# Widening six of 36 weight pieces in the last layer's first block instead of during the experts, and leaving out four unused products of the attention

## The chip, the cores and the metric

One core of a Trainium2 chip. The metric is the device time of one launch in microseconds (us), lower is better. The five engines are named as the profile names them: PE (TensorE, with PEld for its weight loads), DVE (VectorE), ACT (ScalarE), POOL (GpSimd) and SP (SyncE, which here only issues transfers). Each runs its own queue of instructions in order.

## What is computed

Three layers follow one another: a recurrence over 768 positions for 4 sequences and 8 heads of 48 (called the attention), a mixture of 8 experts that takes the best expert of each token, and a gated layer of width 1536.

```python
for t in range(S):                                    # attention
    y[:, :, t] = einsum(r_t, state + u * k_t v_t)
    state = w * state + k_t v_t
for e in range(8):                                    # experts, 384 -> 1024 -> 384
    h = maximum(x[mask] @ w1[e], 0)
    out[mask] = gate_w * eom * (h @ w2[e])
g = x @ w_gate                                        # last layer, 384 -> 1536 -> 384
out = (g * sigmoid(g) * (x @ w_val)) @ w_out
```

The three weight matrices of the last layer arrive as float64. They are 36 pieces of 128 x 384 (12 slices of the width, three matrices each).

## The kernel before

**Attention.** 24 tiles of 128 tokens (6 per sequence), software pipelined, in an order written by hand. For tile `i`, `scaled_k` puts four products in POOL's queue, in this order: two that make `ck` (L455, L456), `kdT` (L458) and `kdc` (L459). `ck` is summed by DVE (`cb`, L478), from `cb` ACT builds the diagonals `dsb` (L482), and PE uses them. `kdc` is read only by `state(i)`, which returns at once for the last tile of a sequence. Loads run three tiles ahead and wait until the tile's buffer has been read.

**Experts.** After the attention a scheduler orders the instructions of each engine by its own estimate of times and by their priority in the program. A step `(e, f)` is 9 products `ph` (x by w1) and, two steps later (`LAG`), 9 products `py` (h by w2). ACT makes the high half of `h` (L1207) and DVE the low half (L1208). Two banks hold `ph`, so the `ph` of step f+2 waits for DVE's `h` of step f. Each step also splits half a group of the raw weights in high and low (ACT L1060, DVE L1063). Expert 0's first 256 tokens are done ahead of the loop (`head`), so that its 8 steps in the loop have only 160 tokens, and a shorter DVE sum `hs` (L1205). From step 10 on, every other step takes a stage of `sorted_positions` (sort tables; DVE L729 to L753, POOL L744 and L749).

**Widening.** `MoE.widen` is a generator. For one piece it loads the two 32-bit halves of each float64 (`cva`, 384 KB), makes a float32 with two ACT operations (L1020, L1021), five of DVE (L1025, L1027, L1030, L1033, L1034) and one of POOL (L1031), and stores it to the DRAM tensor `m32` (L1024, L1040). Three `next` make a piece. `filler(FILLN)` draws two per expert step from step `FILL0` on, and `filler(1000)` draws what is left in step (7, 0).

**Last layer.** `FFN.prepare` is called in step (7, 0). It loads pieces from `m32` (`rw`, L1291) and splits them (L966, L967); `FFN.run` works on blocks of 512 tokens and 12 slices `f`. In the first block slice f+3's pieces are split at slice f. A slice is 18 products `pg` and `pv` (L1356), a sigmoid on ACT (L1360), two DVE products (L1361, L1362), the split of the result in `hh` and `hl` (L966, L967) and 12 products `po` (L1323), which stand on PE behind the `pg` and `pv` of a later slice. The inputs of block 1 go to the pool `xq2`, which is empty during block 0.

Of the kernel before, what the change touches and what calls it, by code (L numbers as in the profile page):

```python
# [9 lines left out]
F32 = mybir.dt.float32  # L10
# [28 lines left out]
def moe_kernel(ctx, tc, cst, small, tok, tr, u, w1, w2, m_gate, m_val, m_out, out):  # L39
# [68 lines left out]
    moe = MoE(tc, outer, env)  # L108
# [197 lines left out]
    with ExitStack() as actx:  # L306
# [132 lines left out]
        def scaled_k(i):  # L439
# [19 lines left out]
            nc.gpsimd.tensor_tensor(out=kdc[:, :, 0:D], in0=k_t, in1=wk_tok, op=ALU.mult)  # L459
# [511 lines left out]
class MoE:  # L971
    def __init__(self, tc, c, env):
# [6 lines left out]
        self.stages = self.widen()  # L979
# [12 lines left out]
    def widen(self):  # L992

        nc, env, cv = self.nc, self.env, self.cv
        DM, KD = env["DM"], env["KD"]
        def load(i):
            a = cv.tile([P, 2 * DM], I32, name="cva", bufs=3)
            f, kind = divmod(i, 3)
            if kind < 2:
                src = (env["m_gate"], env["m_val"])[kind].bitcast(I32).rearrange("(k p) f -> p k f", p=P)  # L1000
                nc.sync.dma_start(
                    out=a.rearrange("p (k f) -> p k f", k=KD), in_=src[:, :, 2 * f * P : 2 * (f + 1) * P]
                )
            else:
                nc.sync.dma_start(out=a, in_=env["m_out"].bitcast(I32)[f * P : (f + 1) * P, :])
            return a

        n = self.F32CH
        loaded = [load(0), load(1)]
        yield  # L1010
        store = None
        for i in range(n):
            if i + 2 < n:
                loaded.append(load(i + 2))
            pair = loaded.pop(0).rearrange("p (n t) -> p n t", t=2)
            ab = cv.tile([P, DM], F32, name="ab", bufs=3)
            bits = ab.bitcast(I32)
            low = cv.tile([P, DM], F32, name="low")
# [7 lines left out]
            ex = cv.tile([P, DM], I32, name="exw")  # L1026
# [11 lines left out]
            if i + 1 < n:  # L1038
                yield
        nc.sync.dma_start(out=env["m32"][n - 1], in_=store)  # L1040
# [196 lines left out]
class FFN:  # L1237
# [25 lines left out]

    def scales(self, ns):
# [6 lines left out]
    def x_tiles(self, n):  # L1271
        start, size = self.blocks[n]
        xh, xl = (self.xq[n % 2].tile([P, self.env["KD"], size], F32R, name=name) for name in ("xh2", "xl2"))
        self.xs[n] = xh, xl, self.scales(slice(start, start + size))
# [28 lines left out]
    def run(self):  # L1303
# [4 lines left out]
        self.xq.append(c.enter_context(tc.tile_pool(name="xq2", bufs=1, reuse_waits="tile")))  # L1308
        self.wts = c.enter_context(tc.tile_pool(name="wts", bufs=1, reuse_waits="tile"))
# [32 lines left out]
        for n, (_, size) in enumerate(blocks):  # L1342
            xh, xl, _ = self.xs.pop(n)
            po = [p_o.tile([P, DM], F32, name=f"po{t}") for t in (range(2, 4) if n == len(blocks) - 1 else range(size // P))]
            for f in range(KF2):
# [20 lines left out]
                if n == 0 and f + self.AHEAD < KF2:  # L1366
                    with tc.issue_after(a), tc.issue_after(b):
                        self.weights(f + self.AHEAD)
                    if f + self.AHEAD + 1 < KF2:
# [26 lines left out]

LAG = 2
# [4 lines left out]
FILL0, FILLN = 2, 2  # L1402
# [98 lines left out]
```

## Time and profile before

| | |
|---|---|
| median of 3 runs | 820.76 us (820.52 to 821.94) |
| the profiled execution, its own time | 828.89 us |
| span in the trace of that execution | 827.1 us |
| PE busy | 790.2 us, 96% |
| DVE busy | 515.1 us, 62% |
| ACT busy | 347.6 us, 42% |
| POOL busy | 210.6 us, 25% |

The profiled execution has its own time, 8.1 us above the median of the runs, and its span covers all but 1.8 us of that. In the trace the attention goes to about 130 us, the head of expert 0 to 150, the loop over the experts from 156 to 370, and the last layer from 370 to 823. An engine's share over the whole span mixes these stages, so the stages are read one by one. PE's busy time is modelled for overlapping products: a busy PE is not PE at its peak.

### The profile page before, as it was taken

The numbers are of one execution on the slowest core, as the hardware profiler recorded it, in microseconds if no ns is written. First come the engines' busy times: TensorE is split into PE (matmuls) and PEld (weight loads), VectorE is DVE, ScalarE is ACT, GpSimd is POOL, SyncE is SP. The second block draws the span as 40 slices with busy tenths as digits, with TensorE's granted clock in tenths as the row PEclk, the third lists the DMA queues.
The fourth block names the chain that finished last, engine by engine and source line by source line (L and its number), as shares of the span: only waits on it lengthen the run. The fifth ranks groups of instructions, "written<-read, shape, count | busy, mean of one in ns | idle before, by whom it ended". The sixth has DMA issues, their size and how long they took to land.

```text
span 827.1 us, 15617 instructions
## 1 busy us (share of the span) xinstructions
PE 790.2 (96%) x5982; PEld 718.5 (87%) x5983; DVE 515.1 (62%) x1091; ACT 347.6 (42%) x791; POOL 210.6 (25%) x207
## 2 busy tenths in 40 slices
PE   7989779699999999999999999999999999999997
PEld 4877678688999999998888888888888888889997
DVE  7789997399999999955554335333533443344443
ACT  5878663364575576554432222212222222122322
POOL 6999951354524422200001000200020020001000
PEclk9999999899999999999999999999999999999999
DMA  8899933686777877342210000000000010001000
GB/s 322 297 361 334 332 128 108 215 268 194 253 222 260 252 245 253 89 139 86 86 59 32 19 1 13 39 0 1 14 39 1 0 45 1 1 7 40 1 20 24
DMA packets 61860, 99.28 MB, mean 120 GB/s; under 512 B 5461, under 2 KB 48105, under 8 KB 61776
## 3 DMA queue, kind: packets, MB, share of 16 engines
q1 hardware_dynamic: 58320, 88.34, 32.3%
q0 software_dynamic: 3456, 9.85, 3.5%
q8 instruction: 49, 0.80, 0.4%
q14 instruction: 35, 0.29, 0.1%
HBM read 81.64 MB, written 16.53 MB: 119 GB/s over the span
## 4 chain that ended last, share of the span: by engine, by line
issue 58%; PE 16%; DVE 4%; POOL 3%; DMA 1%; ACT 1%; POOLq 0%; SPq 0%; ACTq 0%; DVEq 0%
PE ph L1188 7%; PE py L1188 6%; POOL out_dram L1332 2%; PE pya L1188 1%; DMA m<-ab 1%; PE pha L1188 1%; DVE w2l L1063 1%; PE pt L1154 1%; DVE ab L1034 1%; DMA cva<-in_w_gate_dram 0%; DVE exw L1027 0%; PE ph L1184 0%; DVE ab L1030 0%; DVE h L1208 0%; DVE low L1033 0%
## 5 line engine op out<-in xcount | busy, mean ns | idle before, releaser
L1361 DVE TENSOR_TENSOR hv<-pg,hv 128x512 f32<-128x512 f32 (+1 forms) x84 | 51.6, 615 | 153.8 <-ACT hv L1360 153.7
L1332 POOL DMA_INDIRECT out_dram<-ot,tokd x24 | 24.8, 1035 | 448.3 <-DVE ot L1331 443.6
L1360 ACT ACTIVATE hv<-pg 128x512 f32<-128x512 f32 (+1 forms) x84 | 45.1, 537 | 167.4 <-PE pg L1356 167.2
L966 ACT CAST hh<-hv 128x512 fp32r<-128x512 f32 (+1 forms) x84 | 47.0, 560 | 142.1 <-DVE hv L1362 142.1
L1323 PE MATMUL po<-wh,hl 128*128 128x384 f32 x288 | 96.8, 337 | 0.0
L1323 PE MATMUL po<-wh,hh 128*128 128x384 f32 x288 | 96.8, 336 | 0.0
L1323 PE MATMUL po<-wl,hh 128*128 128x384 f32 x288 | 96.8, 336 | 0.0
L1356 PE MATMUL pg<-xh,wh 128*128 128x512 f32 (+1 forms) x252 | 91.2, 362 | 0.0
L1356 PE MATMUL pv<-xh,wl 128*128 128x512 f32 (+1 forms) x252 | 91.1, 362 | 0.0
L1356 PE MATMUL pg<-xh,wl 128*128 128x512 f32 (+1 forms) x252 | 91.1, 361 | 0.0
L1356 PE MATMUL pv<-xh,wh 128*128 128x512 f32 (+1 forms) x252 | 91.0, 361 | 0.0
L1356 PE MATMUL pv<-xl,wh 128*128 128x512 f32 (+1 forms) x252 | 91.0, 361 | 0.0
L1356 PE MATMUL pg<-xl,wh 128*128 128x512 f32 (+1 forms) x252 | 90.7, 360 | 0.0
L1188 PE MATMUL ph<-x,w1h 128*128 128x416 f32 (+6 forms) x336 | 88.3, 344 | 0.0
L967 DVE TENSOR_TENSOR hl<-hv,hh 128x512 fp32r<-128x512 f32 (+1 forms) x84 | 51.7, 616 | 45.8 <-ACT hh L966 45.6
L1362 DVE TENSOR_TENSOR hv<-pv,hv 128x512 f32<-128x512 f32 (+1 forms) x84 | 51.7, 615 | 45.1 <-PE pv L1356 43.6
L1188 PE MATMUL py<-h,w2h 128*128 128x416 f32 (+6 forms) x336 | 79.1, 340 | 0.0
L1031 POOL TENSOR_TENSOR low<-low,exw 128x384 f32<-128x384 f32 x36 | 42.5, 1180 | 114.9 <-DVE exw L1027 73.3
L482 ACT ACTIVATE dsb<-cs,cb 128x128 f32<-128x128 f32 x192 | 58.8, 389 | 25.0 <-DVE cb L478 25.0
L1188 PE MATMUL ph<-x,w1l 128*128 128x416 f32 (+6 forms) x168 | 59.8, 356 | 3.8 <-DVE h L1208 3.1
L1188 PEld LDWEIGHTS ph<-x,w1h 128*128 128x128 f32 x336 | 62.4, 191 | 0.2
L1188 PEld LDWEIGHTS py<-h,w2h 128*128 128x128 f32 x336 | 61.0, 188 | 0.1
(244 smaller groups left out, 1699.0 us busy)
## 6 DMA issues: line engine op xcount, KB each, us to landing
r<-in_w_dram SPq DMA_DIRECT2D x64, 384.0 KB, 4.5
yd_all<-in_tr_dram SPq DMA_DIRECT2D x24, 512.0 KB, 7.5
yd_all<-in_tok_dram SPq DMA_DIRECT2D x24, 384.0 KB, 5.3
m<-ab SPq DMA_DIRECT2D x36, 192.0 KB, 3.8
rw<-m SPq DMA_DIRECT2D x36, 192.0 KB, 2.4
yd_all<-in_tok_dram SPq DMA_DIRECT2D x24, 256.0 KB, 5.9
x_d<-xt SPq DMA_DIRECT2D x24, 192.0 KB, 5.5
cva<-in_w_gate_dram SPq DMA_DIRECT2D x12, 384.0 KB, 4.3
```

The source lines that it names most:

```text
L482: nc.scalar.mul(dsb[:, h, :], ident, cb[:, h : h + 1])
L966: first = nc.scalar.copy(hi, src)
L967: second = nc.vector.tensor_tensor(out=lo, in0=src, in1=hi.bitcast(F32), op=ALU.subtract)
L1031: nc.gpsimd.tensor_tensor(out=low, in0=low, in1=ex.bitcast(F32), op=ALU.mult)
L1034: nc.vector.scalar_tensor_tensor(out=bits, in0=pair[:, :, 1], scalar=-(2**31), in1=low.bitcast(I32), op0=ALU.bitwise_and, op1=ALU.bitwise_or)
L1188: nc.tensor.matmul(dst[:, 0:n], lhsT=a, rhs=b, start=start and t == 0, stop=stop and t == 2)
L1323: mm = nc.tensor.matmul(po[t], lhsT=a[:, t * P : (t + 1) * P], rhs=bb, start=(f == 0 and j == 0), stop=(f == KF2 - 1 and j == 2))
L1332: st = nc.gpsimd.indirect_dma_start(out=out[:, :], out_offset=bass.IndirectOffsetOnAxis(ap=tokd[:, i : i + 1].bitcast(U32), axis=0), in_=o ...
L1356: nc.tensor.matmul(dst, lhsT=a[:, fs], rhs=bb[:, q, :], start=(q == 0 and j == 0), stop=(q == KD - 1 and j == 2))
L1360: nc.scalar.activation(hv, pg, AF.Sigmoid)
L1361: nc.vector.tensor_tensor(out=hv, in0=pg, in1=hv, op=ALU.mult)
L1362: nc.vector.tensor_tensor(out=hv, in0=pv, in1=hv, op=ALU.mult)
```

## The change

Pieces 0 to 29 are widened during the experts, from step 10 on instead of step 2, by the same two `next` per step. Pieces 30 to 35 (slices 10 and 11) are widened by a second generator, which `FFN.run` draws from in slices 0 to 8 of block 0 (two `next` in the first two slices, then three), with the not yet used `xq2` tile as its room: two buffers for `cva` and `ab` in place of three, one for `low` and `exw` in place of two, and one load ahead in place of two. For that, the two tiles of a block's inputs become one tile. The product `kdc` is left out for the last tile of each sequence (tiles 5, 11, 17 and 23).

```diff
--- before.py
+++ after.py
@@ -105,7 +105,7 @@
 
     outer = ctx.enter_context(ExitStack())
     env = locals()
-    moe = MoE(tc, outer, env)
+    env["moe"] = moe = MoE(tc, outer, env)
     sm_t = const.tile([P, small.shape[1]], F32, name="sm_t")
     nc.sync.dma_start(out=sm_t, in_=small)
     wp = sm_t[:, 0:NP]
@@ -456,7 +456,8 @@
                 nc.gpsimd.tensor_tensor(out=ck, in0=ck, in1=r_t, op=ALU.mult)
             if i:
                 nc.gpsimd.tensor_tensor(out=kdT, in0=kT, in1=wkT, op=ALU.mult)
-            nc.gpsimd.tensor_tensor(out=kdc[:, :, 0:D], in0=k_t, in1=wk_tok, op=ALU.mult)
+            if (i + 1) % NCH:
+                nc.gpsimd.tensor_tensor(out=kdc[:, :, 0:D], in0=k_t, in1=wk_tok, op=ALU.mult)
 
         def scaled_r(i):
             if i >= NTILE:
@@ -976,7 +977,9 @@
         w1, w2, self.F32CH = env["w1"], env["w2"], 3 * env["KF2"]
         self.w1v = w1.rearrange("e (k p) f -> e p k f", p=P)
         self.w2v = w2.rearrange("e (f p) d -> e p f d", p=P)
-        self.stages = self.widen()
+        self.stages = self.widen(
+            range(self.F32CH - LATE), lambda name, shape, dtype, bufs: self.cv.tile(shape, dtype, name=name, bufs=bufs), 2
+        )
         self.ahead = {}
         self.pend = []
         self.raws, self.xs, self.ids = {}, {}, {0: slice(0, 1)}
@@ -989,12 +992,12 @@
         for _ in range(n):
             next(self.stages, None)
 
-    def widen(self):
-
-        nc, env, cv = self.nc, self.env, self.cv
+    def widen(self, items, tile, before):
+
+        nc, env = self.nc, self.env
         DM, KD = env["DM"], env["KD"]
         def load(i):
-            a = cv.tile([P, 2 * DM], I32, name="cva", bufs=3)
+            a = tile("cva", [P, 2 * DM], I32, before + 1)
             f, kind = divmod(i, 3)
             if kind < 2:
                 src = (env["m_gate"], env["m_val"])[kind].bitcast(I32).rearrange("(k p) f -> p k f", p=P)
@@ -1005,17 +1008,16 @@
                 nc.sync.dma_start(out=a, in_=env["m_out"].bitcast(I32)[f * P : (f + 1) * P, :])
             return a
 
-        n = self.F32CH
-        loaded = [load(0), load(1)]
+        loaded = [load(i) for i in items[0:before]]
         yield
         store = None
-        for i in range(n):
-            if i + 2 < n:
-                loaded.append(load(i + 2))
+        for i in items:
+            if i + before < items.stop:
+                loaded.append(load(i + before))
             pair = loaded.pop(0).rearrange("p (n t) -> p n t", t=2)
-            ab = cv.tile([P, DM], F32, name="ab", bufs=3)
+            ab = tile("ab", [P, DM], F32, 3)
             bits = ab.bitcast(I32)
-            low = cv.tile([P, DM], F32, name="low")
+            low = tile("low", [P, DM], F32, 2)
 
             nc.scalar.activation(ab, pair[:, :, 1].bitcast(F32), AF.Abs, scale=2.0**-112)
             nc.scalar.activation(low, pair[:, :, 0].bitcast(U32), AF.Copy, scale=2.0**-52)
@@ -1023,7 +1025,7 @@
             if store is not None:
                 nc.sync.dma_start(out=env["m32"][i - 1], in_=store)
             nc.vector.tensor_scalar(out=ab, in0=ab, scalar1=W_MAX, scalar2=None, op0=ALU.min)
-            ex = cv.tile([P, DM], I32, name="exw")
+            ex = tile("exw", [P, DM], I32, 2)
             nc.vector.tensor_scalar(
                 out=ex, in0=bits, scalar1=3, scalar2=0x7F800000, op0=ALU.logical_shift_left, op1=ALU.bitwise_and
             )
@@ -1035,9 +1037,9 @@
                 out=bits, in0=pair[:, :, 1], scalar=-(2**31), in1=low.bitcast(I32), op0=ALU.bitwise_and, op1=ALU.bitwise_or
             )
             store = ab
-            if i + 1 < n:
+            if i + 1 < items.stop:
                 yield
-        nc.sync.dma_start(out=env["m32"][n - 1], in_=store)
+        nc.sync.dma_start(out=env["m32"][i], in_=store)
 
     def load(self, e, g):
         nc, env, GF = self.nc, self.env, 2
@@ -1261,6 +1263,20 @@
         self.warm = self.sbp.tile([P, 1], F32, name="warm")
         nc.vector.memset(self.warm, 0.0)
 
+    def late(self, room):
+
+        moe, DM = self.env["moe"], self.env["DM"]
+        place, used = {}, {"cva": 0, "ab": 4 * DM, "low": 6 * DM, "exw": 7 * DM}
+
+        def tile(name, shape, dtype, bufs):
+            size, bufs = shape[1], {"cva": 2, "ab": 2}.get(name, 1)
+            at = used[name] + place.setdefault(name, 0) % bufs * size
+            place[name] += 1
+            t = room[:, at : at + size]
+            return t if dtype == F32 else t.bitcast(dtype)
+
+        return moe.widen(range(moe.F32CH - LATE, moe.F32CH), tile, 1)
+
     def scales(self, ns):
         sb = self.sbp.tile([P, ns.stop - ns.start], F32, name="sb")
         (self.nc.sync if ns.start else self.nc.gpsimd).dma_start(
@@ -1270,7 +1286,8 @@
 
     def x_tiles(self, n):
         start, size = self.blocks[n]
-        xh, xl = (self.xq[n % 2].tile([P, self.env["KD"], size], F32R, name=name) for name in ("xh2", "xl2"))
+        both = self.xq[n % 2].tile([P, 2, self.env["KD"], size], F32R, name="x2")
+        xh, xl = both[:, 0], both[:, 1]
         self.xs[n] = xh, xl, self.scales(slice(start, start + size))
 
     def x_part(self, n, q):
@@ -1306,6 +1323,7 @@
         KD, KF2, DM, NTILE = (env[x] for x in ("KD", "KF2", "DM", "NTILE"))
         blocks = self.blocks
         self.xq.append(c.enter_context(tc.tile_pool(name="xq2", bufs=1, reuse_waits="tile")))
+        late = self.late(self.xq[1].tile([P, 2, KD, NB], F32, name="x2").rearrange("p a k t -> p (a k t)"))
         self.wts = c.enter_context(tc.tile_pool(name="wts", bufs=1, reuse_waits="tile"))
         wk = c.enter_context(tc.tile_pool(name="wk2", bufs=2, reuse_waits="tile"))
         p_o = c.enter_context(tc.tile_pool(name="q_o", bufs=1, space=PSUM, reuse_waits="tile"))
@@ -1366,6 +1384,8 @@
                 if n == 0 and f + self.AHEAD < KF2:
                     with tc.issue_after(a), tc.issue_after(b):
                         self.weights(f + self.AHEAD)
+                    for _ in range(2 + (f > 1)):
+                        next(late, None)
                     if f + self.AHEAD + 1 < KF2:
                         self.load(f + self.AHEAD + 1)
                 pend.append((n, f, hh, hl, po))
@@ -1394,12 +1414,14 @@
 
 HURRY = 18
 
+LATE = 6
+
 LAG = 2
 
 DIST = 3
 
 POS0, POSK = 10, 2
-FILL0, FILLN = 2, 2
+FILL0, FILLN = 10, 2
```

The lines of the changed kernel are one to 20 higher than those before: L1025 became L1027, L1208 became L1210, L1360 became L1378.

**DVE, the end of expert 0 and the start of expert 1.** `hs` and `h` belong to the steps, `w1l` and `w2l` are the split of raw weights, `x` is the next expert's input; `ab`, `exw` and `low` are the widening. Before:

```order
L1208 SCALAR_TENSOR_TENSOR h<-hs,h 128x160
L1025 TENSOR_SCALAR ab<-ab 128x384
L1063 TENSOR_TENSOR w2l<-r_2773,w2h 128x768
L1027 TENSOR_SCALAR exw<-ab 128x384
L1205 TENSOR_TENSOR hs<-hs,ph 128x160 x2
L967 TENSOR_TENSOR x<-pt,x 128x3x128
L1030 TENSOR_SCALAR ab<-ab 128x384
L967 TENSOR_TENSOR x<-pt,x 128x3x32
L1208 SCALAR_TENSOR_TENSOR h<-hs,h 128x160
L1033 TENSOR_TENSOR low<-ab,low 128x384
L1063 TENSOR_TENSOR w1l<-r_2775,w1h 128x768
```

Now:

```order
L1210 SCALAR_TENSOR_TENSOR h<-hs,h 128x160
L1065 TENSOR_TENSOR w2l<-r_2769,w2h 128x768
L1207 TENSOR_TENSOR hs<-hs,ph 128x160 x2
L1210 SCALAR_TENSOR_TENSOR h<-hs,h 128x160
L968 TENSOR_TENSOR x<-pt,x 128x3x128
L1065 TENSOR_TENSOR w1l<-r_2771,w1h 128x768
L1210 SCALAR_TENSOR_TENSOR h<-hs,h 128x160
L1065 TENSOR_TENSOR w2l<-r_2773,w2h 128x768
L968 TENSOR_TENSOR x<-pt,x 128x3x32
L1207 TENSOR_TENSOR hs<-hs,ph 128x160 x2
L968 TENSOR_TENSOR x<-pt,x 128x3x128
```

The widening's operations are gone from this place; the rest stands in nearly the same order.

**DVE, expert 1's seventh and eighth `h` of 416 columns.** `dsel` is the table of the sort that four POOL products wait for. Before:

```order
L741 TENSOR_TENSOR dsel<-dhif,cs 128x576
L1025 TENSOR_SCALAR ab<-ab 128x384
L1033 TENSOR_TENSOR low<-ab,low 128x384
L1208 SCALAR_TENSOR_TENSOR h<-ph,h 128x416
L1034 SCALAR_TENSOR_TENSOR ab<-cva,low 128x384
L1063 TENSOR_TENSOR w1l<-r_3089,w1h 128x768
L1027 TENSOR_SCALAR exw<-ab 128x384
L1034 SCALAR_TENSOR_TENSOR ab<-cva,low 128x384
L1208 SCALAR_TENSOR_TENSOR h<-ph,h 128x416
```

Now:

```order
L742 TENSOR_TENSOR dsel<-dhif,cs 128x576
L1065 TENSOR_TENSOR w2l<-r_2992,w2h 128x768
L1035 TENSOR_TENSOR low<-ab,low 128x384
L1210 SCALAR_TENSOR_TENSOR h<-ph,h 128x416
L1027 TENSOR_SCALAR ab<-ab 128x384
L1036 SCALAR_TENSOR_TENSOR ab<-cva,low 128x384
L1065 TENSOR_TENSOR w1l<-r_3040,w1h 128x768
L1029 TENSOR_SCALAR exw<-ab 128x384
L1032 TENSOR_SCALAR ab<-ab 128x384
L1210 SCALAR_TENSOR_TENSOR h<-ph,h 128x416
```

The widening has begun here in both (of its operations 37 stand ahead of the last row in the loop's queue before, 13 now). One `h` more now stands between `dsel` and the last row.

**ACT, the first slices of the last layer.** `x_5486` is the room in `xq2`, so its rows are the late pieces; `hv` is the sigmoid, `hh` the high half of the result, `wh` a split weight. Before:

```order
L1360 ACTIVATE hv<-pg 128x512
L966 CAST hh_5615<-hv 128x512
L966 CAST wh_5619<-rw 128x384
L966 CAST wh_5623<-rw 128x384
L966 CAST wh_5627<-rw 128x384
L1360 ACTIVATE hv<-pg 128x512
L966 CAST hh_5661<-hv 128x512
L966 CAST wh_5665<-rw 128x384
```

Now:

```order
L1378 ACTIVATE hv<-pg 128x512
L1022 ACTIVATE x_5486<-x_5486 128x384
L967 CAST hh_5527<-hv 128x512
L967 CAST wh_5531<-rw 128x384
L967 CAST wh_5535<-rw 128x384
L967 CAST wh_5539<-rw 128x384
L1023 ACTIVATE x_5486<-x_5486 128x384
L1378 ACTIVATE hv<-pg 128x512
L1022 ACTIVATE x_5486<-x_5486 128x384
L1378 ACTIVATE hv<-pg 128x512
L967 CAST hh_5577<-hv 128x512
```

A late piece's first operation, which waits for its load, now stands in front of the first slice's `hh`, and another in front of the third slice's sigmoid, behind which the second slice's `hh` stands. Pieces 30 to 32 come before these rows, in the queue of expert 7.

## Rows read from the trace of the kernel before

**Rows 1.** The page, part 2: DVE busy share in 40 slices of 20.7 us, in tenths.
```profile
DVE  7789997399999999955554335333533443344443
```

**Rows 2.** Stretches (us): busy of PE, PEld, DVE, ACT, POOL; granted clock; DMA share; GB/s.
```profile
165.00:208.00 43.00, 38.38 (x221) 36.02 (x220) 41.93 (x87) 24.91 (x55) 22.60 (x20) 1.00 0.74 230
...
222.00:345.00 123.00, 123.00 (x718) 121.12 (x717) 118.08 (x221) 77.28 (x149) 37.46 (x32) 1.00 0.74 232
...
382.00:402.00 20.00, 20.00 (x99) 17.62 (x98) 10.61 (x19) 7.01 (x16) 0.00 (x0) 1.00 0.32 100
```

**Rows 3.** Waits of PE, 165 to 225: releaser, us in total, times, longest.
```profile
PE ph L1188 <- DVE h L1208: 3.1, 2, 2.3
PE pt L1154 <- DVE x L967: 0.8, 1, 0.8
PE ph L1188 <- DVE w2l L1063: 0.4, 1, 0.4
PE py L1184 <- DVE h L1208: 0.3, 1, 0.3
```

**Rows 4.** Timeline of PE, expert 1: start, us, what, [idle before <-releaser].
```profile
208.16 0.71 PE L1188 MATMUL ph<-x,w1l 128*128 128x412 f32 x1 [2.26 <-DVE h L1208]
```

**Rows 5.** Stretches of one us: PEclk is the granted TensorE clock.
```profile
208.00:209.00 1.00, 0.84 (x2) 0.83 (x3) 1.00 (x2) 1.00 (x4) 0.47 (x1) 0.51 0.32 99
...
211.00:212.00 1.00, 1.00 (x5) 0.96 (x5) 1.00 (x3) 0.00 (x0) 0.00 (x0) 0.78 0.97 267
```

**Rows 6.** The chain that ended last: start, us, what, in two experts.
```profile
208.16 3.43 PE ph L1188 x9
...
221.49 1.72 PE ph L1188 x9
```

**Rows 7.** DVE by operation and shape, 225 to 345: count, busy us, mean ns.
```profile
L1063 DVE TENSOR_TENSOR w1l<-r,w1h 128x768 fp32r<-128x768 f32 x18 | 18.4, 1021 | 0.0
L1030 DVE TENSOR_SCALAR ab<-ab 128x384 int32<-128x384 int32 x24 | 17.8, 740 | 0.3
L1033 DVE TENSOR_TENSOR low<-ab,low 128x384 f32<-128x384 f32 x25 | 13.8, 551 | 3.9 <-POOL low L1031 3.6
L1034 DVE SCALAR_TENSOR_TENSOR ab<-cva,low 128x384 int32<-128x384 int32 x24 | 13.2, 552 | 0.3
...
L1025 DVE TENSOR_SCALAR ab<-ab 128x384 f32<-128x384 f32 x24 | 8.5, 354 | 0.2 <-ACT ab L1020 0.2
```

**Rows 8.** Timeline of DVE in front of the wait at 208.
```profile
203.06 1.90 DVE L1063 TENSOR_TENSOR w1l<-r,w1h 128x768 fp32r<-128x768 f32 x1
204.88 1.31 DVE L1027 TENSOR_SCALAR exw<-ab 128x384 int32<-128x384 int32 x1
206.11 1.50 DVE L1034 SCALAR_TENSOR_TENSOR ab<-cva,low 128x384 int32<-128x384 int32 x1
207.53 0.58 DVE L1208 SCALAR_TENSOR_TENSOR h<-ph,h 128x416 fp32r<-128x416 f32 x1
```

**Rows 9.** Timeline of POOL in the same place.
```profile
201.04 1.68 POOL L744 TENSOR_TENSOR dsel<-dsel,cs 128x576 bf16<-128x576 f32 x1 [2.46 <-DVE dsel L741]
202.68 4.51 POOL L749 TENSOR_TENSOR dsel<-dsel,scale 128x576 bf16<-128x576 f32 x3
```

**Rows 10.** Timeline of POOL in the attention: the product of tile 5.
```profile
30.99 1.01 POOL L459 TENSOR_TENSOR kdc<-yd_all 128x384 f32<-128x384 f32 x1
```

**Rows 11.** Waits of DVE, 0 to 130.
```profile
DVE cb L478 <- POOL ck L456: 6.5, 7, 1.6
```

**Rows 12.** Timeline of DVE in the attention: its last such wait.
```profile
55.28 0.55 DVE L478 TENSOR_REDUCE cb<-ck 128x8 f32<-128x384 f32 x1 [0.47 <-POOL ck L456]
```

**Rows 13.** ACT by operation and shape, 225 to 345.
```profile
L1020 ACT ACTIVATE ab<-cva 128x384 f32<-128x384 f32 x24 | 13.5, 561 | 5.4 <-DMA m<-ab 5.4
```

**Rows 14.** The float64 loads (tile cva): time to landing.
```profile
DMA to landing us min/median/max: 3.9/4.6/5.6
```

**Rows 15.** Timeline of PE: first product of the last layer that needs hh.
```profile
381.14 0.34 PE L1323 MATMUL po<-wh,hl 128*128 128x384 f32 x1
```

## The prediction

> **What bounds the kernel now.** I read the share of each engine over time first. DVE is 77 to 99% busy in the front half and 30 to 55% in the back half [rows 1], so work that moves from the experts to the last layer goes from a full place to an emptier one. That helps only where PE waits for DVE. The reader should therefore look at stretches next [rows 2]. From 165 to 208 us PE is busy 38.38 of 43 us and DVE 41.93. From 222 to 345 DVE is as full (118.08 of 123) and yet PE has no gap (123.00). In the last layer PE is full and DVE has 10.61 of 20 us. So DVE costs time only at the start of the loop over the experts, where the short steps of expert 0 and the first sort stages meet the widening. The waits of PE there give the price [rows 3]: 3.1 us for `h` (two waits, 2.3 the longer), 0.8 for the next expert's `x`, 0.4 for `w2l`, 0.3 for `py`'s `h`; 4.6 in all, or about 4.5 from the unrounded waits.
>
> The longest of them costs more than its length. It ends at 208.16 [rows 4]. In the microsecond behind it the granted clock is 0.51, the lower level of 1.2 GHz, and in 211 to 212 it is 0.78 on its way back [rows 5]. The nine products behind the wait took 3.43 us; nine like them at 221.49, at the full clock, took 1.72 [rows 6]. PE thus lost about 1.7 us more after the wait was over.
>
> **The price of a piece.** Its five DVE operations are two of 0.354 us (L1025, and L1027 of the same size), 0.740, 0.551 and 0.552 [rows 7], together 2.55, or 0.51 each. On average 0.15 us of waiting for POOL's L1031 comes with a piece (3.6 us over 25 [rows 7]).
>
> **Part 1: the widening starts at step 10.** By the order of DVE, 37 widening operations stood before expert 1's eighth `h` (the one that ends the 208 wait), and 13 do now. That takes 24 x 0.51 = 12.2 us from the stretch of 165 to 208, leaving DVE with 29.7 of 43 us, 69%. Three of the four kinds of waits lie in expert 0's steps or at the change to expert 1, ahead of the sort tables. There the rest of DVE's queue keeps its order and moves up, so I expect these waits (1.5 us) and the shorter wait for `h` (3.1 - 2.3 = 0.8) to go.
>
> The 2.26 us wait has a cause of its own. In front of it three DVE operations were stretched: 1.90 us for a `w1l` that takes 1.02 elsewhere, 1.31 for an `exw` of 0.354, 1.50 for an L1034 of 0.552 [rows 7, 8]. That is 2.8 us more than their size, and `h` followed at 207.53. All of it lies beside four POOL products on `dsel`, 1.68 us from 201.04 and 4.51 from 202.68 [rows 9]. The change leaves these products in. What it takes away is DVE's arrears: before, DVE came to that place without slack; now it has had 12 us less to do, and can reach each `h` as soon as ACT's half is there. PE then has up to two further groups of nine products, 1.72 us each, before it needs the `h`: about 3.4 us of cover against 2.8 of stretching. One more `h` of 0.58 stands between `dsel` and the eighth, which makes the cover thin: 3.4 against 3.4. I take it that most of the wait goes.
>
> The Trainium skill, page "SBUF — State Buffer", section "SBUF: two separate sides", says that VectorE and GpSimd share a pair of ports as an exclusive lock: a GpSimd operation that has it keeps a VectorE operation with two SBUF inputs out until it ends. The stretched rows agree for the two operations with two inputs; the one-input `exw` was stretched too. By that rule the same four products would hold DVE again at any load, which is the first rival below.
>
> Sum of part 1: of 4.5 us of waits, 4.3 go, and 1.7 of half clock goes with the long one. Bounds: 0.8 + 1.5 = 2.3 without the long wait (then no clock is regained either), and 4.6 + 1.7 = 6.3 with everything.
>
> What is removed from step 2 on must be done by the end. Thirty pieces at the same rate from step 10 fill the rest of the experts as before, where PE does not wait at 96% of DVE [rows 2]. Pieces 30 to 32 stand, by the order, in expert 7's queue still; they cost PE nothing by the same row.
>
> **Part 2: block 0 of the last layer.** In a slice PE has 30 products; 99 take 20 us [rows 2], so a slice is 6.1 us. DVE has 10.61/20 x 6.1 = 3.2 us in it, and a piece adds 2.55 + 0.15: 5.9, still under 6.1. DVE has no room to spare in slices 0 to 2, which hold pieces 33 to 35, but nothing piles up. ACT gets two operations of about 0.56 us [rows 13] to 7.01 of 20: covered. POOL is idle there. Loads and stores go through a queue at a DMA share of 0.32. The cost that is not hidden by any sum is the order on ACT: piece 34's first operation waits for its load and stands ahead of the first slice's `hh`, piece 35's ahead of a sigmoid. Before, the first `po` that needs `hh` began at 381.14 [rows 15]. Piece 34's load needs piece 32's buffer, free about 3 us into the layer by my estimate, 373. With 0.56 for the piece's operation and as much each for `hh` and `hl`, the landing may take 381.1 - 373 - 1.7 = 6.4 us. Such loads took 3.9 to 5.6, median 4.6 [rows 14]. The cover holds by 0.8 at worst. Bounds: 0, and two waits of 0.3 with 1.7 of half clock each, 4.0. I take 0.5, near the low end, because all rows of loads lie inside the cover. Joining two input tiles into one adds a wait only if block 1's inputs are written before the last late piece is stored; block 1 is some 60 us later. Nothing.
>
> **Part 3: four products fewer on POOL.** Each is about 1.01 us [rows 10]. DVE waits for POOL's `ck` seven times, 6.5 us in all [rows 11], the last time at 55.28 for 0.47 [rows 12]. Only tile 5's product, at 30.99, lies ahead of some of these waits; the other three come at or after the last, where DVE sets the pace. So 1.0 us. Bounds: 0, if the next tile's loads set the pace there (the early attention loads are the heaviest of the kernel); and 2, if tile 11's counts also.
>
> **Sum.** 1.0 + 4.3 + 1.7 - 0.5 = 6.5 us. The profiled execution's 828.89 would become 822.4. It is 8.1 above the median; I carry the saving over, not the offset: 820.76 - 6.5 = **814.3**. About 0.2%, 1.6 us, is what a measurement of this kernel can tell from no change.
>
> **The rivals.**
> - *The stall at the sort table stays.* The four POOL products hold DVE whatever its arrears, and one more `h` stands behind them. Then the 2.26 and the 1.7 remain: 6.5 - 4.0 = 2.5 gained, 818.3. For it: the stretching alone is 2.8 us, more than the wait. Against: DVE has 12 us less in front. Chance 0.19.
> - *The waits only move.* From step 10 the widening and the sort stages start together, at the old rate; new waits of 3.5 us with 1.7 of half clock and less take the place of the old, and about 1.0 is left: 819.8, no change. For it: DVE at 96% later on. Against: at that load PE waited for nothing [rows 2]. Chance 0.10.
> - *ACT waits for late loads in block 0; slower.* If piece 34's and 35's loads land after L us, PE idles twice for L - 6.4 and loses 1.7 to the clock each time. Against 7.0 gained elsewhere the break-even is 2 x (L - 6.4 + 1.7) = 7.0, L = 8.2. At twice the median, L = 9.2, the loss is 9.0: 822.8. For it: these operations stand in ACT's own order ahead of `hh`. Against: no such load took over 5.6 [rows 14], and the DMA is less used here. Chance 0.06.
> - *More comes.* Attention 2.0, all of 4.6 and 1.7, and block 0 free: 8.3, 812.5. For it: DVE falls to 69% ahead of these waits, and the late loads lie inside their cover. Against: it takes every upper bound at once. Chance 0.10.
> - *It does not do what it says*: three of the six late pieces stay among expert 7's work, by the order. That alone does not change the sum, since PE does not wait for DVE there.
>
> **How the numbers follow.** The forecast has 0.55, within 812.8 to 816.5 (its parts by 1.5 to 2 either way). The range from 811.5 to 819.3 takes in the forecast, the larger gain and the stall that stays, 0.84 of the chance, less a little at its edges. Faster by over 0.2%: 0.55 + 0.19 + 0.10 less 0.03 for stalls priced too low, 0.81. Within 0.2%: 0.12. Slower: 0.07.
>
> **What would show it.** In the changed profile DVE should be about 70% busy in the stretch ahead of the eighth `h` of expert 1, PE's waits for `h`, `x` and `w2l` there should sum to under 0.5 us, and the clock should stay at 1.00 where it was 0.51. The products L744 and L749 will still stand beside stretched DVE operations; the question is whether `h` comes late behind them. POOL should have four `kdc` fewer, DVE's wait for `ck` about 1 us less. In block 0, PE's first `po` should follow the `pv` before it without a gap, and the late loads should land within 6.4 us. The forecast is wrong if a wait of 2 us for `h` with a clock of 0.5 behind it is still there, or if `po` waits for `hh` in the first three slices.

## The result and the profile after

The changed kernel takes 811.13 us (median of 4 runs, 810.79 to 812.17), the kernel before 821.35 (820.52 to 821.99): a ratio of 0.9883, with a 95% interval of 0.9869 to 0.9897, or 10.2 us less by the medians. The forecast was 6.5 us less. The sign and the place are right; the size was put too low, and the time lies 0.4 us below the range.

| | before | after |
|---|---|---|
| median of the runs | 821.35 us | 811.13 us |
| profiled execution, own time | 828.89 us | 811.29 us |
| span | 827.1 us | 809.5 us |
| PE busy | 790.2 us | 785.2 us (97%) |
| DVE busy | 515.1 us | 509.8 us (63%) |
| POOL busy | 210.6 us | 208.1 us (26%) |

The two profiled executions differ by 17.6 us, which is more than the change does. The one before had a wait of PE of 6.43 us at 150 us that the one after does not have; the first experiment deals with it. Pieces of the program that lie behind that wait can still be compared. PE's timeline shows the first product of expert 1 (416 columns), of expert 3 (404) and of the last layer, and the last product of all. Before:

```profile
172.13 0.45 PE L1188 MATMUL ph<-x,w1l 128*128 128x416 f32 x1 [0.37 <-DVE w2l L1063]
```
```profile
235.06 0.35 PE L1188 MATMUL ph<-x,w1l 128*128 128x404 f32 x1
```
```profile
370.19 0.39 PE L1356 MATMUL pg<-xh,wl 128*128 128x512 f32 x1
```
```profile
821.49 0.34 PE L1323 MATMUL po<-wh,hl 128*128 128x384 f32 x1
```

and after:

```profile
161.52 0.44 PE L1190 MATMUL ph<-x,w1l 128*128 128x416 f32 x1
```
```profile
216.35 0.34 PE L1190 MATMUL ph<-x,w1l 128*128 128x404 f32 x1
```
```profile
352.05 0.40 PE L1374 MATMUL pg<-x,wl 128*128 128x512 f32 x1
```
```profile
803.32 0.34 PE L1341 MATMUL po<-wh,hl 128*128 128x384 f32 x1
```

From expert 1's first product to the last layer's it is 198.06 us before and 190.53 after, 7.53 less, with the same 1102 products in between. Up to expert 3's first product it is 8.10 less (62.93 against 54.83), but 309 products stand there before and 300 after: six transposes `pt` and three `py` more, about 1.2 us at 0.11 and 0.19 each. On equal work it is 6.9 less up to there and 0.6 behind it. The last layer takes 451.30 and 451.27 us: the late pieces cost nothing there.

The waits of PE from 146 to 360 after the change (releaser; us in total, times, longest) answer to [rows 3]:

```profile
PE ph L1190 <- DVE h L1210: 0.3, 1, 0.3
PE pt L1156 <- DMA xg<-x_d,rows: 0.3, 1, 0.3
PE ph L1186 <- ACT yd_all L1234: 0.2, 1, 0.2
```

The stops for `h`, `x` and `w2l` at the start of the loop are gone. The one of 0.3 us for `h` ends at 343.3, in expert 7, 8.7 us ahead of the last layer; before, PE waited 0.31 us for ACT's `h` at 360.6, 9.6 us ahead of it.

The stretches after the change (us; busy of PE, PEld, DVE, ACT, POOL; granted clock; DMA share; GB/s) answer to [rows 2]; the first reaches up to expert 1's eighth `h`, the last two are slices of block 0:

```profile
154.40:190.85 36.45, 36.45 (x222) 35.77 (x222) 31.53 (x64) 22.28 (x49) 19.01 (x16) 1.00 0.72 232
211.00:334.00 123.00, 123.00 (x727) 121.45 (x726) 112.36 (x216) 75.13 (x146) 35.96 (x32) 1.00 0.73 229
358.00:364.00 6.00, 6.00 (x29) 4.95 (x28) 5.92 (x12) 4.00 (x9) 1.02 (x1) 1.00 0.58 163
364.00:370.00 6.00, 6.00 (x30) 5.15 (x29) 6.00 (x12) 2.54 (x6) 1.12 (x1) 1.00 0.33 104
```

Before the eighth `h` PE is busy all the time and the clock is 1.00. In nearly the same piece of the program (221 products of PE, now 222) DVE had 41.93 us of work in 43 us [rows 2]; now it has 31.53 in 36.45.

The wait that the prediction asked about stood behind four POOL products. They are there again, in POOL's timeline after the change (start, us):

```profile
182.97 2.29 POOL L745 TENSOR_TENSOR dsel<-dsel,cs 128x576 bf16<-128x576 f32 x1 [1.35 <-DVE dsel L742]
185.22 4.52 POOL L750 TENSOR_TENSOR dsel<-dsel,scale 128x576 bf16<-128x576 f32 x3
```

and beside them the stretched operations of DVE, between expert 1's seventh and eighth `h`:

```profile
184.16 0.57 DVE L1210 SCALAR_TENSOR_TENSOR h<-ph,h 128x416 fp32r<-128x416 f32 x1
...
185.40 1.50 DVE L1036 SCALAR_TENSOR_TENSOR ab<-cva,low 128x384 int32<-128x384 int32 x1
186.82 1.90 DVE L1065 TENSOR_TENSOR w1l<-r,w1h 128x768 fp32r<-128x768 f32 x1
188.65 1.31 DVE L1029 TENSOR_SCALAR exw<-ab 128x384 int32<-128x384 int32 x1
189.99 0.36 DVE L1032 TENSOR_SCALAR ab<-ab 128x384 int32<-128x384 int32 x1
190.27 0.58 DVE L1210 SCALAR_TENSOR_TENSOR h<-ph,h 128x416 fp32r<-128x416 f32 x1
```

The three operations took 1.50, 1.90 and 1.31 us, to the hundredth what they took before [rows 8], and the eighth `h` began 6.1 us after the seventh (5.9 before, from 201.62 to 207.53). Yet PE did not wait. The products that need this `h` to be done are expert 2's second group of nine:

```profile
191.99 0.35 PE L1190 MATMUL ph<-x,w1l 128*128 128x412 f32 x1
```

They begin 1.1 us after `h` has ended (190.27 + 0.58 = 190.85). Counted from the end of the products that the eighth `h` is made of, it was done after 3.8 us (187.10 to 190.85), and before the change after 8.6 (199.56 to 208.11): the stretching is the same, the arrears in front of it are gone. PE's own order changed a little too: 11 `py` products stand ahead of this group where nine did. Two products are 0.4 us, so with nine the cover would still have held.

### The profile page after: what moved, and what is told of

It is laid out like the page before. It is cut to its first block, busy times and chain, and to the rows that moved or that the text cites. A ratio compares the mean times of both kernels' runs of the same rounds, so it can differ in the third digit from the quotient of the medians.

```text
span 809.5 us, 15599 instructions
## 1 busy us (share of the span) xinstructions
PE 785.2 (97%) x5982; PEld 715.8 (88%) x5983; DVE 509.8 (63%) x1091; ACT 347.6 (43%) x791; POOL 208.1 (26%) x203
## 4 chain that ended last, share of the span: by engine, by line
issue 54%; PE 12%; DVE 8%; POOL 4%; DMA 4%; ACT 1%; POOLq 0%; SPq 0%; DVEq 0%; ACTq 0%
PE ph L1190 5%; PE py L1190 5%; POOL out_dram L1350 2%; DMA m<-x 1%; DVE w2l L1065 1%; DVE ab L1036 1%; DMA xg<-x_d,rows 1%; DMA m<-ab 1%; DVE h L1210 1%; DVE w1l L1065 1%; POOL xg L1142 1%; DVE low L1035 1%; PE pt L1156 1%; POOL low L1033 1%; DMA rw<-m 1%
## 5 line engine op out<-in xcount | busy, mean ns | idle before, releaser
L1374 PE MATMUL pg<-x,wh 128*128 128x512 f32 (+1 forms) x504 | 147.9, 361 | 0.0
L1374 PE MATMUL pv<-x,wh 128*128 128x512 f32 (+1 forms) x504 | 139.1, 361 | 0.0
L1378 ACT ACTIVATE hv<-pg 128x512 f32<-128x512 f32 (+1 forms) x84 | 45.1, 537 | 163.0 <-PE pg L1374 162.7
L1374 PEld LDWEIGHTS pv<-x,wh 128*128 128x128 f32 x504 | 89.8, 188 | 15.6
L1374 PEld LDWEIGHTS pg<-x,wh 128*128 128x128 f32 x504 | 90.2, 188 | 12.5
L1374 PE MATMUL pv<-x,wl 128*128 128x512 f32 (+1 forms) x252 | 91.1, 361 | 0.0
L1374 PE MATMUL pg<-x,wl 128*128 128x512 f32 (+1 forms) x252 | 91.0, 361 | 0.0
L1190 PE MATMUL py<-h,w2h 128*128 128x416 f32 (+6 forms) x336 | 83.0, 341 | 0.0
L1033 POOL TENSOR_TENSOR low<-low,exw 128x384 f32<-128x384 f32 x30 | 33.6, 1119 | 96.0 <-DVE exw L1029 75.5
```

Of the source, the lines that this page charges most:

```text
L1033: nc.gpsimd.tensor_tensor(out=low, in0=low, in1=ex.bitcast(F32), op=ALU.mult)
L1190: nc.tensor.matmul(dst[:, 0:n], lhsT=a, rhs=b, start=start and t == 0, stop=stop and t == 2)
L1374: nc.tensor.matmul(dst, lhsT=a[:, fs], rhs=bb[:, q, :], start=(q == 0 and j == 0), stop=(q == KD - 1 and j == 2))
L1378: nc.scalar.activation(hv, pg, AF.Sigmoid)
```

## The experiments

They ran later, on two chips (11 and 12), and there the kernel before takes 830 us and the changed one 821.6; so they are compared by the ratio to the kernel before on the same chip, and by two distances in their traces that do not depend on where the run begins: X, from expert 1's first product to the last layer's first, and Y, from there to the last product, both read from PE's timeline as above.

| kernel | median us | ratio (95%) | X us | Y us |
|---|---|---|---|---|
| before, first profile | 821.35 | 1 | 198.06 | 451.30 |
| before, again | 831.28 (one run) | | 198.89 | 451.30 |
| changed, first profile | 811.13 | 0.9883 (0.9869 to 0.9897) | 190.53 | 451.27 |
| changed, again | 821.58 | 0.9896 (0.9878 to 0.9915) | 190.51 | 451.26 |
| start at step 2 | 830.47 | 0.9998 (0.9984 to 1.0012) | 197.84 | 451.25 |
| start at step 6 | 826.65 | 0.9949 (0.9930 to 0.9968) | 195.43 | 451.25 |
| no late piece | 830.50 | 0.9998 (0.9976 to 1.0019) | 196.23 | 455.14 |
| three late pieces | 822.11 | 0.9912 (0.9883 to 0.9941) | 193.67 | 451.26 |
| nine late pieces | 821.55 | 0.9895 (0.9866 to 0.9924) | 189.70 | 452.81 |
| no load ahead | 821.96 | 0.9896 (0.9866 to 0.9925) | 190.49 | 451.27 |
| sort ten steps later (before) | 828.59 | 0.9978 (0.9961 to 0.9995) | 196.49 | 451.29 |
| kdc put back | 822.70 | 0.9913 (0.9896 to 0.9930) | 190.83 | 451.26 |
| kdc out for tile 5 alone | 821.41 | 0.9903 (0.9880 to 0.9925) | 191.44 | 451.28 |
| kdc back for tile 5 alone | 823.21 | 0.9914 (0.9894 to 0.9934) | 191.48 | 451.27 |

Times in the expectations are on the scale of the first comparison, 821 us for the kernel before, unless they are differences. Five of the profiles (the changed kernel twice, and the three on kdc) have the same order of instructions on PE, DVE and ACT; their X lies between 190.51 and 191.48, so 1 us of X can be chance, and their Y differ by 0.02. The times of one kernel spread over 3 to 6 us on these chips, so the distances are the finer measure.

### Is the stall at 150 us part of the kernel?

The kernel before and the changed kernel, both unchanged, for a second profile.

> The kernel before, unchanged, for a second profile. Theory A: the 6.43 us in which every engine but POOL stands still at 150 us in the first profile, and the half clock behind it, belong to that one execution (its own time was 8.1 us above the median); this profile shows no such wait, and a span near 819 us. Theory B: the stall is part of every execution and the changed kernel took it away; then the span is near 827 us again with PE idle for about 6 us at 150.

> The changed kernel again, on the same chip as the three below, to compare them with: 811 us, 0.988 of the kernel before.

The timelines of PE, the kernel before and then the changed one:

```profile
156.95 0.63 PE L1184 MATMUL ph<-x,w1h 128*128 128x320 f32 x1 [7.91 <-ACT yd_all L1232]
```
```profile
157.39 0.64 PE L1186 MATMUL ph<-x,w1h 128*128 128x320 f32 x1 [7.92 <-ACT yd_all L1234]
```

Both have it here, so theory A, that it was that one execution, is wrong; and of theory B only the first half holds, because the change did not take it away. It came in every execution profiled in the experiments, and in one of the first two. The first profile before, with 828.89 us of its own, ran as kernels do here; the runs beside it, with 820.8, seem to have run without the stall and the half clock behind it (that they did is inferred from their times; they have no trace). The ratios with and without it, 0.9896 and 0.9883, agree within their intervals.

### Does the start decide, or the number of pieces?

```diff
-FILL0, FILLN = 10, 2
+FILL0, FILLN = 2, 2
```

> The changed kernel with the widening started at step 2 again; 30 pieces still go through the experts and six through the last layer. Theory A (the start decides: the widening's operations in front of the short steps of expert 0 and of the first sort stages): PE's waits of some 5 us between 160 and 210 us and the half clock behind the longest are back, 817 to 820 us. Theory B (what counts is six pieces, 15 us of DVE, less in the experts): as the changed kernel, 811 to 813 us.

The waits of PE from 157 us on, which are those of [rows 3] one for one (the 0.4 us now put down to `hs` instead of `w2l`):

```profile
PE ph L1190 <- DVE h L1210: 3.2, 2, 2.3
PE pt L1156 <- DVE x L968: 0.8, 1, 0.8
...
PE py L1186 <- DVE h L1210: 0.3, 1, 0.3
```

Theory A held: with six late pieces but the old start, X is 197.84, and by the ratio nothing that can be told from noise is left of the gain.

```diff
-FILL0, FILLN = 10, 2
+FILL0, FILLN = 6, 2
```

> The changed kernel with the widening started at step 6 instead of 10 (six late pieces, kdc as changed). Theory A (each step of widening ahead of expert 1's eighth h keeps its share of DVE's arrears): about half of the loop's gain, some 4 us more than the changed kernel, ratio to the kernel before 0.994. Theory B (only the expert 0 steps with their short h are hurt, and the rest was the sort table alone): the 2.4 us stop ahead of expert 2 is gone, the two stops in expert 0 are back: 1 to 2 us more than the changed kernel, ratio 0.991.

Theory A again: 4.9 of 8.4 us of X are lost with half the steps moved. PE has one stop of 2.0 us for `h`, ahead of expert 2's second group of products (at 202.51), and the two short ones in expert 0 do not come back. In front of this `h` DVE's operations are stretched beside the four POOL products again (`w1l` takes 1.91 us), and here DVE still had arrears.

```diff
-LATE = 6
+LATE = 0
```

(and the second generator is left out)

> The changed kernel with no late pieces: all 36 are widened in the experts, from step 10, so that what is left at the last step falls in expert 7. Theory A (the start decides): PE's waits between 160 and 210 us stay gone, and the time is that of the changed kernel plus what the last pieces cost in expert 7: 811 to 815 us. Theory B (six pieces fewer): 816 to 820 us.

The ratio is 0.9998: neither the 811 to 815 of theory A nor the reason of theory B. The stops up to expert 2 are gone, as A says; but everything left is widened in expert 7, and the last layer pays. PE's timeline, ACT's in the same place, and a stretch (columns as above):

```profile
368.51 0.80 PE L1374 MATMUL pg<-x,wl 128*128 128x512 f32 x1 [3.46 <-ACT x L967]
...
380.71 0.50 PE L1374 MATMUL pg<-x,wl 128*128 128x512 f32 x1 [0.78 <-DVE hv L1379]
```
```profile
366.06 0.93 ACT L967 CAST wh<-rw 128x384 fp32r<-128x384 f32 x2 [1.77 <-DMA rw<-m]
367.84 0.62 ACT L967 CAST x<-yd_all 128x512 fp32r<-128x512 f32 x1 [0.86 <-issue]
```
```profile
368.50:374.00 5.50, 5.49 (x13) 4.29 (x14) 3.72 (x8) 3.49 (x9) 0.00 (x0) 0.50 0.65 173
```

PE waits 3.46 us for the last layer's first input `x`. ACT splits it behind two weights (`wh`), and waits 1.77 us for their reload from `m32` (`rw<-m`), which follows the store of the last piece; another 0.86 us of ACT's idle time has no releaser in the profile. Behind the wait PE runs with a granted clock of 0.50 up to 374. So the late start and the late pieces are one change in two halves: the start takes the stops away, the late pieces keep the bill from falling due at the other end. X and Y together are 9.6 us worse than the changed kernel's.

```diff
-LATE = 6
+LATE = 3
```

> The changed kernel with three late pieces: 33 are widened in the experts from step 10. Without any late piece the end of expert 7 and block 0 gave back some 9 us. Theory A (in proportion: 15 us of DVE for six pieces is 1.5 us of time for each): 4 to 5 us more than the changed kernel, ratio 0.994 to 0.996. Theory B (only the last pieces, whose store and reload the last layer's weights wait for, cost; three fewer give the slack): 0 to 2 us more, ratio 0.988 to 0.992.

X is 3.2 us longer, between the two theories; the ratio lies in theory B's range, and its interval just reaches A's. PE waits twice for `h` ahead of `py` at the end of expert 7, 1.2 us, and 1.0 for `h` at 343.7; block 0 is untouched. The first three pieces put off are worth 6.4 us (9.6 less 3.2) and the next three 3.2.

```diff
-LATE = 6
+LATE = 9
...
-                    for _ in range(2 + (f > 1)):
+                    for _ in range(3 + (f > 1)):
```

> The changed kernel with nine late pieces instead of six and one draw more in each slice of block 0. Theory A (DVE has room for one piece in a slice of block 0: 5.92 and 6.00 us busy of 6.00 in the changed kernel's slices 1 and 2): PE stops in block 0, because hl comes late; 1 to 4 us more than the changed kernel. Theory B (block 0 has room, later slices take it up): no stop of PE, the same time as the changed kernel within 0.5 us.

Y is 1.5 us longer than with six: theory A. X is 0.8 shorter, and the 0.3 us that PE waited for `h` in expert 7 are gone, so the six-piece kernel still pays a little there. PE's waits from 160 to 420 are now in block 0 alone, and the stretches show which slices:

```profile
PE po L1341 <- DVE hl L968: 1.0, 2, 0.5
```
```profile
373.00:379.00 6.00, 6.00 (x30) 5.27 (x29) 5.98 (x12) 2.98 (x7) 1.11 (x1) 1.00 0.65 182
379.00:385.00 6.00, 5.48 (x27) 4.51 (x26) 5.47 (x12) 3.68 (x8) 1.02 (x1) 1.00 0.74 232
385.00:391.00 6.00, 5.50 (x27) 4.56 (x26) 5.88 (x12) 2.93 (x7) 1.13 (x1) 1.00 0.33 101
```

With six pieces DVE is 5.92 and 6.00 of 6.00 us busy in two slices and can rest after them (4.99 in the next); with nine it stays full for four, from 367 to 391, and `hl` comes 0.5 us late twice. Six to nine is about what fits: by their times the two versions cannot be told apart.

### Does ACT's order cost anything in block 0?

```diff
-        return moe.widen(range(moe.F32CH - LATE, moe.F32CH), tile, 1)
+        return moe.widen(range(moe.F32CH - LATE, moe.F32CH), tile, 0)
```

> The changed kernel with no load ahead in the late pieces: each float64 load is issued when its piece is drawn, so that ACT, in whose queue the piece's first operation stands, waits for the whole landing. Theory A (the cover predicted for ACT's order: hh needs the landing under 6.4 us, and these loads take 2 to 5.4): PE waits for nothing, the same time as the changed kernel within 0.7 us. Theory B (the order on ACT is the risk of this change): ACT idles 3 us or more in front of a sigmoid or hh of slices 0 to 2, PE stops for 1 us or more at a po or a pg, 2 to 6 us more.

ACT's timeline shows the first operations of the last three late pieces, each waiting for its own load:

```profile
368.31 0.55 ACT L1022 ACTIVATE x<-x 128x384 f32<-128x384 f32 x1 [1.58 <-DMA x<-in_w_gate_dram]
...
371.78 0.56 ACT L1022 ACTIVATE x<-x 128x384 f32<-128x384 f32 x1 [2.00 <-DMA x<-in_w_val_dram]
...
376.30 0.56 ACT L1022 ACTIVATE x<-x 128x384 f32<-128x384 f32 x1 [1.27 <-DMA x<-in_w_out_dram]
```

ACT waits 1.3 to 2.0 us for each of the three, and neither X nor Y moves: theory A. With the load ahead it waits 1.7 to 1.9, but for something else; in the changed kernel:

```profile
354.68 0.54 ACT L1022 ACTIVATE x<-x 128x384 f32<-128x384 f32 x1 [1.90 <-DMA m<-x]
...
357.81 0.56 ACT L1022 ACTIVATE x<-x 128x384 f32<-128x384 f32 x1 [1.66 <-DMA m<-x]
...
363.18 0.56 ACT L1022 ACTIVATE x<-x 128x384 f32<-128x384 f32 x1 [1.85 <-DMA m<-x]
```

The releaser there is the store of an earlier piece (`m<-x`), whose buffer `ab` the operation overwrites, not the load. The prediction named the wrong transfer, but the cover for it held: the first `po` began at 363.25, 11.2 us into the layer, against 381.14 less 370.19, 10.95, before.

### Are the POOL products to blame for the 2.26 us wait?

In the kernel before:

```diff
-POS0, POSK = 10, 2
+POS0, POSK = 20, 2
```

> The kernel before with the stages of the sort ten steps later (from step 20), so that the four POOL products on dsel do not stand in front of expert 1's eighth h. Theory A (that wait came from DVE's arrears and these products together): the 2.26 us wait and the half clock behind it go, the shorter waits of expert 0 stay: 816 to 818 us. Theory B (the arrears of DVE alone make the wait): it stays within 1 us of its size and the time is within 1 us of the kernel before.

```profile
PE ph L1188 <- DVE h L1208: 2.8, 4, 1.2
PE pt L1154 <- DVE x L967: 0.8, 1, 0.8
```

The long wait is gone, and four short ones for `h`, the longest 1.2 us, stand in its place, one of them (at 243) again just behind the products. X is 1.6 to 2.4 us shorter and the ratio 0.9978, less than theory A's 3 to 5 us. So by this run the products turn arrears into one long stop, and without them the arrears show in other places. The changed kernel is the counterpart: the products stretch DVE as before and PE does not stop.

### What is kdc worth?

```diff
-            if (i + 1) % NCH:
-                nc.gpsimd.tensor_tensor(out=kdc[:, :, 0:D], in0=k_t, in1=wk_tok, op=ALU.mult)
+            nc.gpsimd.tensor_tensor(out=kdc[:, :, 0:D], in0=k_t, in1=wk_tok, op=ALU.mult)
```

> The changed kernel with the four kdc products put back (the widening as changed). Theory A (the milestones of the two traces: 1.0 us by tile 5's product and 0.9 more by tile 17's): 1.9 us more than the changed kernel. Theory B (tile 5 alone, as predicted): 1.0 us more.

and, in two more kernels, `if i != 5:` and `if (i + 1) % NCH or i == 5:` in place of the condition.

> The changed kernel, with kdc left out for tile 5 alone. Theory A: 0.9 us more than the changed kernel, and the start of the last tile's work on PE near 112 us later by as much. Theory B: the same time as the changed kernel.

> The changed kernel, with kdc put back for tile 5 alone. Theory A: 1.0 us more than the changed kernel; the gain at tile 17 stays. Theory B (the gain of tile 5 is what makes the later one possible): 1.9 us more.

By the medians, 1.1 us more with all four put back, 0.2 less with tile 5 alone left out, 1.6 more with tile 5 alone put back. The intervals overlap, so the times alone do not settle it. The traces help for tile 5. DVE's waits for POOL's `ck`, after the change against [rows 11],

```profile
DVE cb L479 <- POOL ck L456: 5.5, 6, 1.6
```

are one fewer and 1.0 us shorter in the first pair of profiles. The number holds in all of them: seven waits in each of the five that compute tile 5's product (6.5 to 8.1 us), two to six in the nine that don't. Their length does not: 0.9 to 7.3 us, and 7.3 is the changed kernel's second profile. PE begins the sixteenth of its 24 groups of products `psy<-dsb` between 83.6 and 83.9 us in the five (median 83.8). In the nine it is 81.3 to 82.9 in seven, 84.2 and 84.6 in two, median 82.3. At the last group the medians are 125.5 and 124.4. So 1.5 us by the medians are won up to there and 1.1 are left at the end, with a spread of 2 us and more; the 1.9 us by which the first two profiles differ at the end of the attention are within it. Theory A of these three (1.9, of which 0.9 by tile 17) is not borne out: with tile 5 alone left out the time is that of the changed kernel, though an interval of some 2 us either way does not exclude the 0.9.

## Why the prediction was right, and where its sum was short

**The place and the mechanism: right.** The stops at the start of the loop went, the clock stayed up, and the runs with the start at step 2 and 6 brought them back, in full and in part. The cause is DVE's arrears and not the POOL products alone: the first rival, that the stall at the sort table stays, fell in the profile after. The Trainium skill, page "SBUF — State Buffer", section "SBUF: two separate sides", calls the shared port an exclusive lock. The trace agrees with the lock (1.50 and 1.90 us for two operations with two inputs beside the products). The one-input `exw` was stretched as well (1.31 us), which the lock for two inputs does not explain. The lock did not decide, because the `h` behind it was done 1.1 us before PE needed it.

**The term that was mis-sized: 4.3 + 1.7 us for the experts.** X alone fell by 7.5 and 8.4 us in the two pairs of profiles, and expert 0, which lies ahead of X, gave about 1.1 more, so the term measured 8.6 to 9.5 us instead of 6.0. In the first pair the stops within X had 0.26, 0.77, 0.84 and 2.26 us of idle time, 4.1, and with 1.7 of half clock 5.8. What the sum left out is that a short stop costs PE more than its idle time. The page counts idle time from the modelled end of the product before. By PE's timeline before the change,

```profile
200.69 0.73 PE L1188 MATMUL py<-h,w2l 128*128 128x416 f32 x3
202.25 0.46 PE L1188 MATMUL ph<-x,w1l 128*128 128x412 f32 x1 [0.84 <-DVE h L1208]
202.55 0.54 PE L1188 MATMUL ph<-x,w1h 128*128 128x412 f32 x2
202.93 0.35 PE L1188 MATMUL ph<-x,w1l 128*128 128x412 f32 x1
```

two products go in 0.38 us (202.55 to 202.93), 0.19 each. The three that began at 200.69 thus used the array to 201.26, and the next began at 202.25, 0.99 us later, where 0.84 is shown as idle. And the first product after the stop took 0.30 us to the next start. That is 0.26 us beyond the idle time; the other two short stops in X cost about as much more, some 0.8 for the three. The long stop was priced rightly:

```profile
205.18 0.73 PE L1188 MATMUL py<-h,w2l 128*128 128x416 f32 x3
208.16 0.71 PE L1188 MATMUL ph<-x,w1l 128*128 128x412 f32 x1 [2.26 <-DVE h L1208]
208.67 0.89 PE L1188 MATMUL ph<-x,w1h 128*128 128x412 f32 x2
...
211.42 1.34 PE L1188 MATMUL py<-h,w2h 128*128 128x416 f32 x6
```

From 205.75 to 208.16 are 2.41 us, and the nine products from there took 3.26 up to the next start instead of 1.69, so 3.98 in all, against 2.26 + 1.7. Of the 1.7 us missing in the first pair, 0.8 are thus the short stops and some 0.6 lie behind expert 3's first product, where no term of the sum looked; the rest stays open. The second pair's kernel before had one stop more and a longer one in expert 7.

Expert 0's share can be read from the first product behind the stall at 150 us to expert 1's first, where 102 products stand in every profile. Where the half clock behind the stall lasts some 4 us, the stretch takes 15.69 and 15.64 us with the widening from step 2 (the kernel before and the run with that start), and 14.38 to 14.70 in four profiles with the start at step 10. That is about 1.1 us, where two waits of 0.3 and 0.4 were shown as idle.

**DVE at 69% before the eighth `h`: wrong as a share.** The work came out nearly as predicted, 31.53 us against 29.7, but the stretch shrank with it, from 43 to 36.45 us, so DVE is 86% busy. A share forecast for a stretch that the change shortens needs the new length.

**Block 0, 0.5 us: 0.** Y is 451.27 against 451.30. DVE's 5.9 us a slice came out (5.92 and 6.00), which is the edge: nine pieces pass it. The third rival, ACT behind late loads, did not come, even with no load ahead; ACT's waits of 1.7 to 1.9 us were for stores, which the prediction had not counted, and they stayed inside the cover.

**Attention, 1.0 us: right within what can be told.** The medians (1.1 us with all four products put back) and the traces point to tile 5's product; the intervals alone do not show it.

**The second rival**, waits that only move behind step 10, did not come: PE has no wait from 161 to 343 us. What no rival named: without the late pieces the gain is given back whole in expert 7 and at the start of the last layer, a place that the prediction took to be free ("they cost PE nothing"). Even pieces 30 to 32 are not quite free there, by the 0.8 us of X that nine late pieces take away.

**The carried offset.** The profile's 828.89 was taken as the ordinary course plus 8.1 us that stay. The traces show what these were: a stall, 6.43 us there and 6.4 to 7.9 in the profiles that have it, with half clock behind it. Both kernels have it, and one profile of the changed kernel does not. The 3 among DVE's high digits in [rows 1] is this stall, which the prediction passed over. Carrying the saving and not the offset was right.

## What to carry to other kernels

Work that is off the critical path still has a best place: look for the stretch where the engine that carries it has just released the bound engine late, and move it from there, but follow it to its deadline, because the same work in front of the next stage can give everything back. Price a stop of PE by the distance between starts on either side, and by the clock behind it, not by the idle time alone. Before two distances are compared, count the work in each: here nine products had moved across one of the marks. How much fits in the new place is read from one stretch: an engine at 6.00 of 6.00 us in two slices still costs nothing if slack follows, and does when the slices become four.

## What was not expected of the hardware

At the end of expert 0's head, in front of the loop, ACT, DVE and PE stand still for 6 to 8 us in all profiled executions but one (13 of 14), in both kernels, while POOL goes on and the DMA engines are full. ACT's timeline of the changed kernel, second profile:

```profile
154.09 0.37 ACT L1234 COPY yd_all<-pya 128x256 f32<-128x256 f32 x1 [6.58 <-remote]
156.96 0.65 ACT L1234 COPY yd_all<-pya 128x256 f32<-128x256 f32 x2 [2.50 <-remote]
```

ACT's copies, whose inputs PE had finished, start 6.6 and 2.5 us late; the profile names no instruction that released them ("remote"). In the first profile of the kernel before it puts two of these copies down to the landing of loads of raw weights (`r<-in_w_dram`, 5.11 and 1.03 us); whether that is the cause was not tested. In the first profile after the change, nothing of the kind is there at 146 to 160 us, with the DMA just as busy (its share from 150 to 158 us is 1.06, against 1.05 in the second). Why an execution has it or not stays open; no run tried to take it away. It is 8 us, nearly as much as the whole change, and it sits in the path of both kernels.
